# The last step of a fused attention and mixer kernel: blocks, writes and reads in another order, and one batch's products dealt otherwise

## The chip, the cores and the metric

The kernel runs on one core of one Trainium2 chip. The metric is device time in microseconds (us). The core has five engines, each with its own stream of instructions: TensorE (PE in the profile, its weight loads PEld), VectorE (DVE), ScalarE (ACT), GpSimd (POOL) and SyncE (SP). They meet through semaphores. SyncE and ScalarE also issue DMA transfers (SPq and ACTq in the profile); [...].

## The reference

For 8 batches and 8 heads, with a sequence of 576 and heads of 64, attention keeps the 32 largest scores of each row; then a mixer follows.

```python
scores = scale * np.matmul(q, k.transpose(0, 1, 3, 2))
kth = np.partition(scores, -top_k, axis=-1)[..., -top_k:-top_k + 1]
scores = np.where(scores >= kth, scores, -1000000000.0)
attn = np.exp(scores - np.max(scores, axis=-1, keepdims=True))
attn = attn / (np.sum(attn, axis=-1, keepdims=True) + 1e-09)
o = np.matmul(attn, v)
x = o.transpose(0, 2, 1, 3).reshape(B, S, H * D)          # 8 x 576 x 512
h = x.transpose(0, 2, 1) @ U @ V                          # rank 32 over the sequence
u = x + h.transpose(0, 2, 1)
out = u + np.maximum(u @ w_ch1, 0.0) @ w_ch2              # 512 -> 2048 -> 512
```

## The kernel before, in words

**Pairs, tiles and steps.** Two heads are a pair g (0 to 31, four to a batch). A pair has five tiles of rows: t = 0 to 3 with 128 rows, for both heads, and the tail t = 4 with the last 64 rows of both. From pair 4 on, tiles 3 and 4 share a step. So `steps` has 132 entries (`STEPS`), step 131 being tiles (31,3) and (31,4), and the big loop over n runs to 133: steps 132 and 133 are a drain, in which only the later stages of the last tiles are left.

**A tile's way.** Scores are made on TensorE (L350) a step ahead. `front` finds the 32nd largest score with VectorE's maximum and replace instructions; it is a generator whose stages the loop calls with `next(here)` in its own step and `next(last)` in the next: ScalarE computes what is to be masked (L571), GpSimd subtracts it (L572), ScalarE takes the exponentials with their sums (L453) and adds a small number to the sums, `den` (L582). `blocks` then turns a tile: VectorE transposes 32 x 32 blocks into `y` (L598), SyncE writes `y` to DRAM as `away` in four transfers (L604), and `back` has ScalarE issue the read of `away` into `PT` (L613), which completes the transposition. The tail is turned on TensorE by `turns` (L634, L639), with ScalarE's copies out of PSUM (L635, L640). `values` multiplies by v (L708, L711; the tail L682), two steps after the tile's own step in the drain (`weighted(n - 2)`), three steps after it otherwise, and ScalarE copies the result to `XT` (L720, L689).

**Sums and mixing.** `inverse` has VectorE invert a pair's sums (L651), transpose them (L653) and SyncE write them to DRAM as `rd` in four transfers (L657); `scale` has ScalarE issue two reads that spread them over partitions (L668). `mixed` multiplies a pair's values by these factors on GpSimd (L740, L743), transposes them (L750, L761), multiplies by U (L773) and V (L785), and GpSimd adds the result to `uT` (L801). It is a generator that goes on by one yield in each fill; its argument `wait` is the number of fills between L761's copy and L773.

**Fills.** `fill` deals out TensorE work of the mixer's two layers: it advances the mixing by one yield and then adds a share to `due` and takes products from `fillers` until the share is used up. In the drain the share is 1.02 and a product of 256 columns counts 0.5, so that a fill is two products, three now and then. `mlp(b)` makes a batch's products in two parts of columns: chunks 0, 1 and 4 (320 columns), then 2 and 3 (256 columns, `lo > 0`); each has 64 products of the first layer (L845) and, for each of four output chunks c, 16 of the second (L862). When 16 are done, ScalarE copies the sum (L873), GpSimd adds `uT` (L874), and `later(12, turned_back(...))` puts the store off by 12 products: TensorE transposes (L886), ScalarE copies (L888), SyncE stores (L892). Batch 6 (`B - 2`, the seventh) is the one in work during the drain; at the start of step 132's second fill, all that is left of it is c = 1, 2 and 3 of its second part, 48 products. The last batch, 7, is done after the drain by `closing`, in a form with fewer products but sums and differences on GpSimd (L931 to L934) and VectorE (L963 to L966); its products are at L938. It is called when pair 31's mixing has ended.

**Order in the drain.** [...] In step 132: fill, values of (31,1), fill, the exponentials of (31,3)'s first half, read of (31,2)'s blocks, two fills, the exponentials of (31,3)'s second half and of (31,4) with the sums, fill, inversion and reading of the factors, values of (31,2), fill, blocks of (31,3), two fills. In step 133: fill, tail's transposes, fill, read of (31,3)'s blocks, three fills, values of (31,3) and (31,4), and the mixing of pair 31 in the fills that follow.

Of the kernel before, what the change touches and what calls it, by code (L numbers as in the profile page):

```python
# [8 lines left out]
F32 = mybir.dt.float32  # L9
# [17 lines left out]
def kernel(  # L27
# [28 lines left out]
    nc = tc.nc  # L56
    B, H, S, D = q.shape
    P = 128
# [4 lines left out]
    NT, TAIL = 4, 64  # L63
    MAIN = NT * P
    HALF = S // 2
    assert S == MAIN + TAIL and D == 64 and H % 2 == 0 and C == 512 and TOPK % 8 == 0
    NPAIR = H // 2
    NP = B * NPAIR

    CH = NT + 1  # L70
    ALONE = NPAIR * CH
# [4 lines left out]
    BLK = 32  # L76
# [8 lines left out]
    mlpp = ctx.enter_context(tc.tile_pool(name="mlpp", bufs=2))  # L85
# [44 lines left out]
    def rows(t):  # L130
        return P if t < NT else TAIL
# [7 lines left out]
    def half(h):  # L139
        return slice(h * D, (h + 1) * D)  # L140
# [324 lines left out]
    def eased(g, t):  # L465
        return bool(ways(g, t)[2])

    def front(tiles):


# [139 lines left out]
    def back(g, t):  # L610

        if (g, t) in aways:
            nc.scalar.dma_start(  # L613
                PTs[g, t].rearrange("p a n -> p (a n)"),
                aways.pop((g, t)).rearrange("p a n -> p (a n)"),
            )
# [26 lines left out]
    def inverse(g, lo, hi):  # L643
        den = dens[g][:, lo:hi]
        if g == NPAIR - 1:
            nc.vector.tensor_scalar_add(den, den, 1e-9)
        if g < NPAIR:
            nc.vector.reciprocal(den, den)
            return
        inverted.add(g)  # L650
        nc.vector.reciprocal(upright[:, 0 : 2 * NT + 1], den)  # L651
        turned_ = small.tile([P, BLK], F32, tag="rows", name="rows", bufs=1)
        nc.vector.transpose(turned_, upright)  # L653
        rd = dram.tile([2 * NT + 1, P], F32, tag="rd", name="rd")
        scales[g] = rd
        for a in range(4):
            nc.sync.dma_start(  # L657
                rd[:, a * BLK : (a + 1) * BLK], turned_[a * BLK : a * BLK + 2 * NT + 1]
            )

    def scale(g):

        rd = scales.pop(g)
        sc = attn.tile([P, TAIL + S], F32, tag="scale", name="scale", bufs=1)
        scales[g] = sc
        flat = rd.rearrange("r n -> () (r n)")
        for h in range(2):
            nc.scalar.dma_start(  # L668
                sc[half(h), (1 - h) * TAIL : (1 - h) * TAIL + S],
                flat[:, h * S : (h + 1) * S].to_broadcast([D, S]),  # L670
            )
# [140 lines left out]
    def later(wait, job):  # L812

        posts.append((ticks + wait, job))

    def tick():

        nonlocal ticks
        ticks += 1
        if posts and posts[0][0] <= ticks:  # L820
            posts.pop(0)[1]()

    def first_layer(cc, f):

        at_ = f * P % W1Q
        return w1s[f * P // W1Q][:, cc, at_ : at_ + P]

    def mlp(b):

        uT = uTs[b]  # L830
        for chunks, (lo, hi) in zip(PARTS, SPAN):
            w = hi - lo
            hTs, phs = [], {}
            order = [(f, cc) for f in range(NF) for cc in range(NC)]
            if lo == 0:
                early = NC - 1
                order[0 : 2 * NC] = [(f, cc) for f in range(2) for cc in range(early)] + [
                    (f, early) for f in range(2)
                ]
            for f, cc in order:  # L840
                while cc == NC - 1 and b not in whole:
                    yield 0
                if cc == 0:
                    phs[f] = ps_m.tile([P, C], F32, tag="mm", name="mm")
                nc.tensor.matmul(  # L845
                    phs[f][:, 0:w],
                    lhsT=first_layer(cc, f),
                    rhs=uT[:, cc, lo:hi],
                    start=(cc == 0),
                    stop=(cc == NC - 1),  # L850
                )
                tick()
                if cc == NC - 1:
                    if f % 2 == 0:
                        hT = mlpp.tile([P, 2, WIDE], F32, tag="hT", name="hT", bufs=HT)
                        hTs += [hT[:, 0], hT[:, 1]]
                    nc.scalar.activation(hTs[f][:, 0:w], phs.pop(f)[:, 0:w], AF.Relu)  # L857
                yield w / C
            for c in range(NC):
                po = ps_m.tile([P, C], F32, tag="mm", name="mm")  # L860
                for f in range(NF):
                    nc.tensor.matmul(  # L862
                        po[:, 0:w],
                        lhsT=w2[:, f, c * P : (c + 1) * P],
                        rhs=hTs[f][:, 0:w],
                        start=(f == 0),
                        stop=(f == NF - 1),
                    )
                    tick()
                    if f < NF - 1:  # L870
                        yield w / C
                oT = mlpp.tile([P, WIDE], F32, tag="oT", name="oT")
                nc.scalar.copy(oT[:, 0:w], po[:, 0:w])  # L873
                nc.gpsimd.tensor_tensor(oT[:, 0:w], oT[:, 0:w], uT[:, c, lo:hi], ALU.add)  # L874
                later(12, turned_back(b, chunks, lo, c, oT))
                yield w / C

    def turned_back(b, chunks, lo, c, oT):


        def run():
            cs = slice(c * P, (c + 1) * P)
            tp = ps_t.tile([P, 3, P], F32, tag="tp", name="tp")
            for i, t in enumerate(chunks):
                n = rows(t)
                nc.tensor.transpose(tp[0:n, i, :], oT[:, OFF[t] - lo : OFF[t] - lo + n], ident)  # L886
            ob = mlpp.tile([P, 3, P], F32, tag="ob", name="ob", bufs=2)
            nc.scalar.copy(ob[:, 0:2], tp[:, 0:2, :])  # L888
            if NT in chunks:
                nc.scalar.copy(ob[0:TAIL, 2], tp[0:TAIL, 2, :])  # L890
            t = chunks[0]
            nc.sync.dma_start(  # L892
                out[b, 0:MAIN, cs].rearrange("(p t) c -> p t c", t=NT)[:, t : t + 2, :],
                ob[:, 0:2],
            )
            if NT in chunks:
                nc.sync.dma_start(out[b, MAIN:S, cs], ob[0:TAIL, 2])

        return run
# [259 lines left out]
    STEPS = len(steps)  # L1159
# [5 lines left out]
    fillers, mixing, due = [], [], 0.0  # L1165

    def fill(k=1):


        nonlocal due  # L1170
        for _ in range(k):
            if passes:
                passes.pop(0)()
            if mixing and next(mixing[0], True):
                mixing.pop(0)
            part = share * (LONG if len(tiles(n)) > 1 else 1)
            if n <= ALONE + BATCH + 2:
                part *= EARLY[min(max(n - ALONE, 0) // NT, NT - 1)]
            due += part
            while due > 0:  # L1180
                if not fillers:
                    due = 0.0
                    break
                done = next(fillers[0], None)
                if done is None:
                    fillers.pop(0)
                elif not done:
                    due = 0.0
                else:
                    due -= done  # L1190

    def tiles(n):

        return steps[n] if 0 <= n < STEPS else []

    def weighted(m):

        for g, t in tiles(m):
            values(g, t)
        if tiles(m)[-1][1] == NT:  # L1200
            mixing.append(mixed(g, None, 1 if g > NPAIR + 1 else 4) if m < STEPS - 1 else mixed(g, 5, 0))

    def turn():

        for _ in tiles(n - 2):
            next(turning, None)

    def turned(n):

        for g, t in tiles(n):  # L1210
            yield from turns(g, t)
# [3 lines left out]
    t = 0  # L1215
# [5 lines left out]
    for n in range(STEPS + 2):  # L1221
        if n < STEPS:
            g, t = steps[n][0]
# [8 lines left out]
        else:  # L1232
            t = NT
# [81 lines left out]
                scores(*tile_, len(tiles(n + 1)) > 1)  # L1315
            fold(*tile_)
        turn()
        fill()
        turn()
        next(last, None)  # L1320
        for tile_ in tiles(n - 2):
            back(*tile_)
        fill()
        turn()
        fill()
        next(last, None)
        if n < STEPS and n - 2 >= ALONE and len(tiles(n - 2)) > 1:
            scale(steps[n - 2][0][0])
        next(here, None)
        if g == NPAIR:  # L1330
# [1 line left out]
        fill()  # L1332
        if n >= STEPS:
            if n == STEPS:
                inverse(NP - 1, 0, 2 * NT + 1)
                scale(NP - 1)
            weighted(n - 2)
        next(here, None)
        for tile_ in tiles(n + 1):
# [4 lines left out]
            if shared(*tile_):  # L1344
                blocks(*tile_)
        turning = turned(n - 1)
        if n < STEPS and n - 1 >= ALONE and len(tiles(n - 1)) > 1:
            owed.append(steps[n - 1][0][0])
            if owed[0] > NPAIR + 1:
                inverse(owed.pop(), 0, 2 * NT + 1)  # L1350
# [45 lines left out]
```

## Time and profile before

| what | us |
|---|---|
| median of 3 runs | 1650.82 (1650.72 to 1653.34) |
| the profiled execution | 1653.27 |
| its span, first to last instruction | 1651.5 |
| TensorE busy | 1558.9 (94%) |
| VectorE busy | 1543.5 (93%) |
| ScalarE busy | 993.8 (60%) |
| GpSimd busy | 1009.1 (61%) |
| values of (31,1), (31,2), (31,3) begin | 1503.62, 1510.31, 1520.86 |
| closing products of batch 7 begin | 1535.60 |
| last product ends | about 1646 |

A line of instructions in order of time gives start, duration, engine, line of the source, operation, what it writes and reads with their shapes, and how many such instructions are merged in it; in brackets at the end stands how long the engine was idle before it and what ended the wait. Rows of digits are the busy share in tenths, in 40 equal slices of the span. A matrix product in 32-bit floats shows as two records. ACTq and SPq lines are the issue of a DMA, not its transfer.

### The profile page before, as it was taken

The numbers are of one execution on the slowest core, as the hardware profiler recorded it, in microseconds if no ns is written. First come the engines' busy times: TensorE is split into PE (matmuls) and PEld (weight loads), VectorE is DVE, ScalarE is ACT, GpSimd is POOL, SyncE is SP. The second block draws the span as 40 slices with busy tenths as digits, with TensorE's granted clock in tenths as the row PEclk, the third lists the DMA queues.
The fourth block names the chain that finished last, engine by engine and source line by source line (L and its number), as shares of the span: only waits on it lengthen the run. The fifth ranks groups of instructions, "written<-read, shape, count | busy, mean of one in ns | idle before, by whom it ended". The sixth has DMA issues, their size and how long they took to land.

```text
span 1651.5 us, 30266 instructions
## 1 busy us (share of the span) xinstructions
PE 1558.9 (94%) x9656; PEld 1185.5 (72%) x9656; DVE 1543.5 (93%) x4388; ACT 993.8 (60%) x2481; POOL 1009.1 (61%) x881
## 2 busy tenths in 40 slices
PE   4566799999999999999999999999999999999998
PEld 2344466788667877788777877788777877787776
DVE  7999999999999999999999999999999999994452
ACT  4888787665665556565666656565655556563320
POOL 4888767756666666665666566656666565653720
PEclk7787799999999999999999999999999999999999
DMA  3333331145445455555545455555545455543001
GB/s 89 100 99 99 88 83 36 42 113 136 135 120 146 126 142 145 134 135 132 138 120 143 129 140 142 140 134 132 137 121 143 128 140 137 142 125 100 7 1 28
DMA packets 278959, 187.06 MB, mean 113 GB/s; under 512 B 174128, under 2 KB 259984, under 8 KB 278800
## 3 DMA queue, kind: packets, MB, share of 16 engines
q1 hardware_dynamic: 258576, 116.44, 29.3%
q10 hardware_dynamic: 20224, 68.69, 13.1%
q8 instruction: 76, 1.25, 0.3%
q14 instruction: 83, 0.68, 0.1%
HBM read 115.31 MB, written 69.73 MB: 112 GB/s over the span
## 4 chain that ended last, share of the span: by engine, by line
PE 72%; DVE 13%; POOL 5%; ACT 4%; DMA 2%; SPq 1%; issue 1%; DVEq 0%; ACTq 0%; POOLq 0%
PE mm L862 22%; PE mm L845 21%; PE sc L350 7%; PE O L711 6%; DVE m L539 4%; DVE upper L534 3%; PE mm L938 3%; PE up L785 2%; PE tp L938 2%; PE sc L938 2%; PE sc L382 2%; PE O L708 1%; PE tp L634 1%; DVE first L521 1%; DVE upper L502 1%; POOL E L544 1%
## 5 line engine op out<-in xcount | busy, mean ns | idle before, releaser
L845 PE MATMUL mm<-uT,w 128*128 128x320 f32 (+1 forms) x1792 | 461.1, 408 | 2.6 <-POOL uT L801 2.1
L862 PE MATMUL mm<-hT,w 128*128 128x320 f32 (+1 forms) x1792 | 460.6, 408 | 0.0
L572 POOL TENSOR_TENSOR Ssb<-Ssb,E 128x576 f32<-128x576 f32 x243 | 339.7, 1418 | 192.4 <-ACT E L571 192.4
L845 PEld LDWEIGHTS mm<-uT,w 128*128 128x128 f32 x1792 | 333.1, 190 | 102.5 <-issue 9.6
L862 PEld LDWEIGHTS mm<-hT,w 128*128 128x128 f32 x1792 | 332.0, 190 | 91.6 <-issue 9.8
L539 DVE MAX8 m<-upper 128x8 f32<-128x304 f32 (+1 forms) x774 | 362.5, 509 | 0.7
L534 DVE MATCH_REPLACE8 upper<-m,upper 128x304 f32<-128x304 f32 (+1 forms) x516 | 256.6, 504 | 0.0
L449 POOL TENSOR_TENSOR lower<-lower,upper 128x576 uint32<-128x576 uint32 x108 | 152.4, 1411 | 135.9 <-DVE upper L448 134.0
L446 POOL TENSOR_TENSOR lower<-Ssb 128x576 uint32<-128x576 uint32 x108 | 152.4, 1411 | 125.6 <-ACT Ssb L395 60.7
L453 ACT ACTIVATE Ssb<-Ssb,nmax 128x576 f32<-128x576 f32 x258 | 201.8, 784 | 18.2 <-POOL Ssb L545 9.2
L350 PE MATMUL sc<-qkT 64*128 64x288 f32 (+1 forms) x1056 | 178.5, 460 | 8.8 <-ACT Ssb L404 7.6
L571 ACT ACTIVATE E<-Ssb,least 128x576 f32<-128x576 f32 x243 | 176.2, 768 | 4.2
L502 DVE MAX8 upper<-lower 128x8 f32<-128x288 f32 x432 | 171.8, 438 | 1.7 <-POOL lower L449 1.7
L395 ACT COPY Ssb<-sc 128x576 f32<-128x576 f32 x216 | 127.5, 642 | 72.7 <-PE sc L350 72.6
L598 DVE STREAM_TRANSPOSE y<-Ssb 128x512 f32<-128x512 f32 (+1 forms) x306 | 150.9, 543 | 0.0
L711 PE MATMUL O<-PT,va 128*64 128x128 f32 x2048 | 144.2, 284 | 0.0
L857 ACT ACTIVATE hT<-mm 128x320 f32<-128x320 f32 (+1 forms) x224 | 91.1, 407 | 82.5 <-PE mm L845 76.9
L350 PEld LDWEIGHTS sc<-qkT 64*128 64x128 f32 (+1 forms) x1056 | 95.4, 196 | 49.8 <-issue 18.0
L711 PEld LDWEIGHTS O<-PT,va 128*64 128x64 f32 x2048 | 112.9, 140 | 16.2 <-issue 1.6
L720 ACT COPY XT<-O 128x128 f32<-128x128 f32 x128 | 33.9, 265 | 107.2 <-PE O L711 100.4
L534 DVE MATCH_REPLACE8 upper<-first,upper 128x304 f32<-128x304 f32 x216 | 97.5, 458 | 0.0
L500 DVE MATCH_REPLACE8 lower<-upper,lower 128x288 f32<-128x288 f32 x216 | 93.9, 442 | 0.0
(268 smaller groups left out, 2270.9 us busy)
## 6 DMA issues: line engine op xcount, KB each, us to landing
away<-y SPq DMA_DIRECT2D x408, 144.0 KB
PT<-away ACTq DMA_DIRECT2D x102, 576.0 KB
raw<-in_moe_w_ch_dram SPq DMA_DIRECT2D x32, 512.0 KB
va<-in_v_dram SPq DMA_DIRECT2D x64, 128.0 KB
scale<-rd ACTq DMA_DIRECT2D x56, 144.0 KB
out_dram<-ob SPq DMA_DIRECT2D x59, 128.0 KB
ld<-in_q_dram SPq DMA_DIRECT2D x108, 64.0 KB
ld<-in_k_dram SPq DMA_DIRECT2D x108, 64.0 KB
```

The costliest lines, as they stand in the source:

```text
L350: nc.tensor.matmul(out, lhsT=qkT[half(h), 0, cols(t)], rhs=qkT[half(h), 1, lo:hi], start=True, stop=True,)
L446: nc.gpsimd.tensor_tensor(bottom, a.bitcast(U32), b.bitcast(U32), ALU.add)
L449: nc.gpsimd.tensor_tensor(bottom, bottom, top.bitcast(U32), ALU.subtract)
L453: nc.scalar.activation(E, chunk, AF.Exp, bias=nmax, scale=SCALE, accum_out=total)
L502: nc.vector.max(spot, lower)
L534: nc.vector.match_replace(nxt, ms[c], curs[c], NEG)
L539: nc.vector.max(ms[c], curs[c])
L571: nc.scalar.activation(gap, chunk, AF.Relu, bias=least[:, c : c + 1], scale=-WIDEN)
L572: nc.gpsimd.tensor_tensor(chunk, chunk, gap, ALU.subtract)
L711: nc.tensor.matmul(O[half(h)], lhsT=va[:, h, j, :], rhs=PT[:, NT * h + j], start=False, stop=(j == NT - 1),)
L845: nc.tensor.matmul(phs[f][:, 0:w], lhsT=first_layer(cc, f), rhs=uT[:, cc, lo:hi], start=(cc == 0), stop=(cc == NC - 1),)
L862: nc.tensor.matmul(po[:, 0:w], lhsT=w2[:, f, c * P : (c + 1) * P], rhs=hTs[f][:, 0:w], start=(f == 0), stop=(f == NF - 1),)
```

## The change

The order of the drain's work is changed, and the stores of batch 6's last part.

- In step 132 the read of (31,2)'s blocks comes after all exponentials, two more fills stand ahead of (31,2)'s values, and the inversion of pair 31's sums comes after the blocks of (31,3). The factors are read in step 133, after (31,3)'s blocks.
- In step 133 three fills are left out (`pace` does nothing there), and the mixing of pair 31 waits 3 fills instead of 5 ahead of its product with U.
- In batch 6's second part of columns, the store of c = 0 is put off by 20 products instead of 12. Those of c = 1, 2 and 3 are turned by VectorE in blocks of 32 x 32 and stored by eight transfers each (`blocked_store`), in place of two transposes on TensorE, a copy on ScalarE and one transfer.

```diff
-                later(12, turned_back(b, chunks, lo, c, oT))
+                later(20 if b == B - 2 and lo > 0 and c == 0 else 12, turned_back(b, chunks, lo, c, oT))
...
+    def blocked_store(b, c, chunks, ob, at_=0):
+
+        for a in range(4):
+            cs = slice(c * P + a * BLK, c * P + (a + 1) * BLK)
+            for i, t in enumerate(chunks):
+                nc.sync.dma_start(
+                    out[b, 0:MAIN, cs].rearrange("(m i t) c -> t i m c", i=BLK, t=NT)[t],
+                    ob[a * BLK : (a + 1) * BLK, at_ + i * P : at_ + (i + 1) * P].rearrange(
+                        "i (m c) -> i m c", c=BLK
+                    ),
+                )
+
     def turned_back(b, chunks, lo, c, oT):
         def run():
+            if b == B - 2 and lo > 0 and c > 0:
+                ob = mlpp.tile([P, 3 * P], F32, tag="ob", name="ob", bufs=2)
+                nc.vector.transpose(ob[:, 0 : 2 * P], oT[:, 0 : 2 * P])
+                blocked_store(b, c, chunks, ob)
+                return
...
+    def pace():
+
+        if n <= STEPS:
+            fill()
...
-            mixing.append(mixed(g, None, 1 if g > NPAIR + 1 else 4) if m < STEPS - 1 else mixed(g, 5, 0))
+            mixing.append(mixed(g, None, 1 if g > NPAIR + 1 else 4) if m < STEPS - 1 else mixed(g, 3, 0))
...
         turn()
-        fill()
+        pace()
         turn()
         next(last, None)
-        for tile_ in tiles(n - 2):
-            back(*tile_)
-        fill()
+        if n != STEPS:
+            for tile_ in tiles(n - 2):
+                back(*tile_)
+        pace()
         turn()
-        fill()
+        pace()
         next(last, None)
-        if n < STEPS and n - 2 >= ALONE and len(tiles(n - 2)) > 1:
+        if n == STEPS:
+            for tile_ in tiles(n - 2):
+                back(*tile_)
+        if n - 2 >= ALONE and len(tiles(n - 2)) > 1:
             scale(steps[n - 2][0][0])
...
             if n == STEPS:
-                inverse(NP - 1, 0, 2 * NT + 1)
-                scale(NP - 1)
+                fill(2)
             weighted(n - 2)
...
-        if n < STEPS and n - 1 >= ALONE and len(tiles(n - 1)) > 1:
+        if n - 1 >= ALONE and len(tiles(n - 1)) > 1:
             owed.append(steps[n - 1][0][0])
             if owed[0] > NPAIR + 1:
                 inverse(owed.pop(), 0, 2 * NT + 1)
```

## The prediction

> **What bounds the kernel now.** I read the page first, then TensorE's instructions in order of time through the drain (loop steps 132 and 133, about 1503 to 1536 us), then ScalarE's and SyncE's there, then busy time by stretch. From the page, the busy shares and the end of the chain by line:
>
> ```profile
> PE 1558.9 (94%) x9656; PEld 1185.5 (72%) x9656; DVE 1543.5 (93%) x4388; ACT 993.8 (60%) x2481; POOL 1009.1 (61%) x881
> PE   4566799999999999999999999999999999999998
> DVE  7999999999999999999999999999999999994452
> ```
>
> VectorE is full until slice 37 and idle half of the time after it; TensorE is full to the end. Nothing in the diff acts before step 132, so only the drain and what follows can move. TensorE there:
>
> ```profile
> 1503.62 0.39 PE L708 MATMUL O<-PT,vd 128*128 128x128 f32 x2
> ...
> 1504.95 4.15 PE L862 MATMUL mm<-hT,w 128*128 128x256 f32 x18
> 1510.31 0.49 PE L708 MATMUL O<-PT,vd 128*128 128x128 f32 x2 [1.20 <-DMA PT<-away]
> ...
> 1515.53 0.60 PE L634 MATMUL tp<-ident,Stail 128*128 128x128 f32 x4
> ...
> 1516.07 3.62 PE L862 MATMUL mm<-hT,w 128*128 128x256 f32 x16
> 1520.86 0.46 PE L708 MATMUL O<-PT,vd 128*128 128x128 f32 x2 [1.17 <-DMA PT<-away]
> ```
>
> A product of batch 6 (256 columns) is two records: 16 records in 3.62 us, of which 0.17 is the last one's modelled tail, make 0.431 us per product. Counted so, TensorE is free at 1504.95 + 9 x 0.431 = 1508.83 and starts tile (31,2)'s values at 1510.31: wait A, 1.48 us. It is free again at 1516.07 + 8 x 0.431 = 1519.52 and starts (31,3)'s at 1520.86: wait B, 1.34 us. Both are for blocks read back from DRAM. A third, wait C, stands at the head of batch 7's closing products:
>
> ```profile
> 1540.75 1.13 PE L938 MATMUL mm<-Stail,raw 128*128 128x288 f32 x4
> 1542.48 0.44 PE L886 MATMUL tp<-ident,oT 128*128 128x128 f32 x2 [0.59 <-POOL oT L874]
> ```
>
> The closing products start at 1535.60; the 12 up to 1542.48 need 12 x 0.485 = 5.82 us, so 1.06 us is lost (0.76 at the store's transpose, 0.30 before it). After that the stretch 1542.5 to 1647.5 has TensorE busy 104.45 of 105 us. The end is therefore TensorE's work plus A + B + C = 3.88 us, and this is nearly all that can be won. What ScalarE does between:
>
> ```profile
> 1506.79 0.33 ACTq L613 DMA_DIRECT2D PT<-away  x1
> 1507.17 0.78 ACT L453 ACTIVATE Ssb<-Ssb,nmax 128x576 f32<-128x576 f32 x1 [1.06 <-POOL Stail L572]
> ...
> 1508.83 0.30 ACT L582 ACTIVATE den<-den,eps 128x9 f32<-128x9 f32 x1
> 1511.97 1.12 ACTq L668 DMA_DIRECT2D scale<-rd  x2
> ...
> 1516.64 0.27 ACT L640 COPY PTt<-tp 128x128 f32<-128x128 f32 x1
> 1517.07 0.32 ACTq L613 DMA_DIRECT2D PT<-away  x1
> ```
>
> ScalarE stands until 1506.79 for the write of (31,2)'s blocks, and the exponential that (31,3)'s blocks need starts only then. VectorE inverts the sums at 1509.16 to 1509.62 and transposes the blocks at 1509.59 to 1511.09; SyncE issues the sums' rows, then the blocks.
>
> [...]read (31,3) is issued at 1517.07, just after its blocks landed at 1516.97. [...]in step 129 the read at 1471.90 precedes the start (1472.13) of the copy L640 that the program has ahead of it. [...]here reads of blocks took 2.1 to 3.0 us of packets, alone or with other traffic.
>
> **The change part by part.**
>
> *Read (31,2)* goes behind the exponentials of (31,3) and the tail. The last of these that waits is the tail's, for GpSimd's subtraction, which ends at 1506.84. I put the issue at 1507.1 (before: 1506.79); the bound, if it has to stand behind the sums' addition, is 1508.1. Issue to first product took 3.52 us, so it is ready at 1510.62, or 1510.75 with the next blocks' write beside it.
>
> *Two fills* before these values: 4 products more, so TensorE arrives at 1504.95 + 13 x 0.431 = 1510.55. Wait A becomes 0.2 us: -1.28. Bounds of A: 0 and 1.2.
>
> *Blocks (31,3).* Their exponential no longer waits: 1506.1 to 1506.97 (0.87 as before). VectorE transposes at 1507.05 to 1508.55, SyncE issues 4 writes by 1510.4, and with 3.7 us from transpose to landing (1502.96 to 1506.64 for (31,2)), and up to 1.2 for the collision with the read, they land by 1513.5, 3.5 us earlier. The inversion (0.43 us of VectorE) and 4 row writes (1.35 us of SyncE) come after: rows land by 1514. Batch 6's first late store is put off to the 20th product, so it can't stand in SyncE ahead of them.
>
> *Read (31,3)* doesn't get these 3.5 us. In step 133 it stands on ScalarE behind the copies L635 and L640 of tile (31,4), which wait for TensorE's transposes L634 and L639, and these stand behind three fills of step 132 and one of step 133. TensorE: 1510.75 + 1.44 (values) + 8 x 0.431 + 0.22 (the put-off store's two transposes) = 1515.86. From L634 to the read took 0.88 to 0.94 us in the steps before (1470.96 or 1471.02, by the modelled start, to 1471.90), so 1516.74. From issue to first product, 3.79 us as before: 1520.53. Three fills are gone from step 133, so TensorE is there at 1515.86 + 0.54 + 2 x 0.431 = 1517.26. Wait B becomes 3.27 us: +1.93. Bounds 2.7 to 3.9. The stall that the earlier write should cure moves behind a transpose.
>
> *Factors.* Their read (2 DMAs) now follows read (31,3). In step 129 its packets end 4.7 us after the block read's issue, so it lands about 5.0 after: 1521.75. GpSimd then needs 2.16 us for four multiplications, 1523.9; TensorE wants the result at 1520.53 + 2.0 + 4 x 0.431 = 1524.25. The slack is 0.3 us; I charge +0.2, bounds 0 and 1.5.
>
> *Batch 6's stores c = 1 to 3*: 6 transposes at 0.11 leave TensorE, -0.66, and 3 copies (0.37) ScalarE. Added are three VectorE transposes of 256 columns, about 0.43 each (0.48 for 288 columns in L1123), where VectorE is otherwise idle 22.9 us, and 24 writes of 16 KB, about 0.43 us of SyncE each, where SyncE has nothing queued from 1544 to 1608. Nothing on the path. If that cover were gone, 3 x 8 x 0.43 = 10.3 us of SyncE would delay later stores.
>
> *Wait of 3 instead of 5 fills, three fills fewer in step 133.* The products aren't removed: 11 instead of 5 stand after the mixing's last transforms. So 2.6 us more of cover for GpSimd's sums and VectorE's differences, which bound the closing's head: wait C goes, -1.06; bounds -0.5 and -1.06. The copies between (1.4 us) still fit in 3 fills (2.6 us).
>
> Sum: -1.28 + 1.93 + 0.2 - 0.66 - 1.06 = -0.87. The profiled execution took 1653.27 us (span 1651.5 and 1.8 around it), so it would be 1652.4; its runs had a median of 1650.82, which gives **1649.9 us**. With the bounds of all terms: -1.48 + 1.36 - 0.66 - 1.06 = -1.84 to -0.28 + 2.56 + 1.5 - 0.66 - 0.5 = +2.6, so 1649.0 to 1653.4 is the forecast's own range. 0.2% (3.3 us) is about what a measurement of this kernel tells from no change; runs before already spread 2.6.
>
> **Rivals.**
>
> *Both block waits vanish* (0.12). If ScalarE gives out read (31,3) as soon as the blocks have landed (1513), it is ready at 1516.8, before TensorE's 1517.26. B is then 0: -1.28 - 1.34 - 0.66 - 1.06 = -4.3, 1646.5 us. For it speaks that reads overtake queued copies; against it, that I find no read that passes an instruction still waiting for its semaphore.
>
> *A stays* (0.14). The read is issued at 1508.1, ready at 1511.7: A is 1.1 and all after it moves by 0.9; 1650.8 us. [...]for it, that four queued instructions are more than the usual lead.
>
> *The factors' read becomes the bound: slower* (0.08). Place: TensorE at transpose L750, for GpSimd's multiplications. Each us that the factors land after about 1522.0 costs one. Slower by over 0.2% needs 4.2 us beyond that, 1526.2, over 9 us after the issue. For it: the read was ahead by half a step and hidden, and now it is behind 576 KB in its own queue, beside a 128 KB store. Against it: in step 129 the pair is done in 5 us. It would give 1654.5 or more.
>
> *The forecast itself* has 0.66.
>
> **How the numbers follow.** The forecast and "A stays" both lie within 0.2%: 0.80 same. Faster is the first rival, 0.12; slower the third, 0.08. The range of 8 in 10 leaves out most of the first and third and takes in the bounds short of their joint extremes and the spread of runs: 1647.4 to 1652.6.
>
> **What would show it.** Right: read (31,2) at about 1507 and A under 0.5; writes of blocks (31,3) from about 1508.6; read (31,3) some 0.9 us after L634, and B near 3.3, the longest idle time of TensorE in the drain; closing products from about 1535.8 with no wait after. Wrong: a read issued before L634 (B gone); L750 waiting for GpSimd; closing products that still wait for sums, or VectorE idle behind a store's transposes.

## The result and the profile after

The changed kernel takes 1654.68 us (median of 13 runs, 1653.35 to 1656.53), the kernel before 1650.97 (13 runs). The ratio is 1.0019, with a 95% interval of 1.0010 to 1.0027: slower by 3.7 us, of which the interval leaves 1.7 to 4.5. The forecast was 1649.9, and 1654.68 lies outside its range of 1647.4 to 1652.6.

The two profiled executions reach the drain at different times: the values of (31,1) begin at 1503.62 before and at 1501.41 after, and the change does nothing ahead of step 132. So all that follows is counted from there. From there to the first closing product it is 31.98 us before and 35.92 after, +3.94; to the end of the span 147.88 and 150.39, +2.51. TensorE after, in order of time; the lines that were 708, 634, 750 still are, the closing's L938 is now L955:

```profile
1501.41 0.38 PE L708 MATMUL O<-PT,vd 128*128 128x128 f32 x2
...
1502.75 5.88 PE L862 MATMUL mm<-hT,w 128*128 128x256 f32 x26
1510.02 0.49 PE L708 MATMUL O<-PT,vd 128*128 128x128 f32 x2 [1.39 <-DMA PT<-away]
...
1515.24 0.60 PE L634 MATMUL tp<-ident,Stail 128*128 128x128 f32 x4
...
1515.79 1.03 PE L862 MATMUL mm<-hT,w 128*128 128x256 f32 x4
1520.59 0.67 PE L708 MATMUL O<-PT,vd 128*128 128x128 f32 x2 [3.77 <-DMA PT<-away]
1521.18 1.98 PE L711 MATMUL O<-PT,va 128*64 128x128 f32 x16
...
1537.33 1.13 PE L955 MATMUL sc<-uT,w 128*128 128x288 f32 x4
```

Wait A, counted as in the prediction: TensorE is free at 1502.75 + 13 x 0.431 = 1508.35 and starts at 1510.02, 1.67 us (1.48 before). Wait B: free at 1515.79 + 0.86 = 1516.65, starts at 1520.59, 3.94 us (1.34 before). And something that before doesn't have: the 16 records of L711 take 1.98 us instead of 1.09, and both tiles' values 3.57 us (1520.59 to 1524.16) instead of 2.00. Busy time by stretch shows why; the columns are the stretch, its length, the busy time of PE, PEld, DVE, ACT and POOL with their instructions, then the granted clock, DMA share and GB/s:

```profile
1517.34:1520.75 3.41, 0.16 (x1) 0.19 (x2) 0.00 (x0) 0.00 (x0) 0.00 (x0) 0.99 0.78 235
1520.75:1524.16 3.41, 3.41 (x38) 3.07 (x38) 0.00 (x0) 0.27 (x1) 0.69 (x1) 0.51 0.15 48
```

After a stretch of 3.41 us in which TensorE was busy for 0.16, the granted clock is half for as long again. The closing products have lost wait C: the first 12 of them run from 1537.33 on at their 0.97 us per four records (two products), with no idle time. ScalarE after, and GpSimd's first use of the factors:

```profile
1505.57 0.30 ACT L582 ACTIVATE den<-den,eps 128x9 f32<-128x9 f32 x1
1505.71 0.33 ACTq L613 DMA_DIRECT2D PT<-away  x1
...
1515.88 0.58 ACT L635 COPY PTt<-tp 128x512 f32<-128x512 f32 x1 [0.50 <-PE tp L634]
1516.13 0.33 ACTq L613 DMA_DIRECT2D PT<-away  x1
1516.36 0.27 ACT L640 COPY PTt<-tp 128x128 f32<-128x128 f32 x1
1516.62 4.34 ACTq L668 DMA_DIRECT2D scale<-rd  x2
```

```profile
1523.47 1.43 POOL L740 TENSOR_TENSOR uT<-XT,scale 128x256 f32<-128x256 f32 x2 [9.23 <-DMA scale<-rd]
```

The sum to the first closing product: A +0.19, B +2.60, values +1.57, the products after them +0.1, the transposes gone from this stretch -0.44: +4.0, and +3.94 is measured. From the closing on the prediction's working has wait C and the last two transposes, -1.06 - 0.22 = -1.28, so +2.7 for +2.51 measured.

### The profile page after: what moved, and what is told of

Same layout as the page of the kernel before. It is cut to its first block, busy times and chain, and to the rows that moved or that the text cites. A ratio compares the mean times of both kernels' runs of the same rounds, so it can differ in the third digit from the quotient of the medians.

```text
span 1651.8 us, 30279 instructions
## 1 busy us (share of the span) xinstructions
PE 1556.6 (94%) x9650; PEld 1183.9 (72%) x9650; DVE 1543.9 (93%) x4391; ACT 992.9 (60%) x2478; POOL 1009.5 (61%) x881
## 4 chain that ended last, share of the span: by engine, by line
PE 72%; DVE 22%; DMA 2%; issue 1%; SPq 1%; ACT 1%; DVEq 0%; ACTq 0%
PE mm L862 22%; PE mm L845 22%; DVE m L539 7%; DVE upper L534 7%; PE sc L350 7%; PE O L711 6%; PE mm L955 3%; DVE first L521 2%; PE tp L955 2%; PE sc L955 2%; PE up L785 2%; PE sc L382 2%; DMA PT<-away 2%; PE O L708 1%; PE tp L634 1%; DVE upper L502 1%
## 5 line engine op out<-in xcount | busy, mean ns | idle before, releaser
L711 PE MATMUL O<-PT,va 128*64 128x128 f32 x2048 | 143.7, 284 | 0.0
L711 PEld LDWEIGHTS O<-PT,va 128*64 128x64 f32 x2048 | 112.4, 140 | 16.1 <-issue 1.3
```

Of the source, the lines that this page charges most:

```text
L711: nc.tensor.matmul(O[half(h)], lhsT=va[:, h, j, :], rhs=PT[:, NT * h + j], start=False, stop=(j == NT - 1),)
```

## The experiments

Every ratio is against the kernel before, run on the same chip at the same time. "Changed" stands for the changed kernel, +3.7 us.

**TensorE kept busy in wait B.** 30 transposes that nobody reads, ahead of the values of (31,3):

```diff
             if n == STEPS:
                 fill(2)
+            else:
+                spin = ps_s.tile([P, 2, 512], F32, tag="sc", name="sc")
+                for _ in range(30):
+                    nc.tensor.transpose(spin[:, 0, 0:P], ident, ident)
             weighted(n - 2)
```

> The changed kernel, with 30 transposes of the identity into an unused accumulator (about 3.3 us of TensorE work that nobody reads) ahead of the values of (31,3) in step 133, so that TensorE does not stand still while it waits for the read. Theory 1 (the long wait makes the granted clock drop to half, and the values then run at half speed): no half-clock stretch in the drain, values of (31,3) and (31,4) take 2.0 us instead of 3.57, still starting about 19.2 us after the values of (31,1); the run is 1.6 us faster than the changed kernel, so about 2 us slower than before. Theory 2 (the transfers that run at that time slow the values): they still take about 3.5 us, and the time stays that of the changed kernel, 3.7 us over before.

Measured: 1653.03 us for 1650.85, ratio 1.0015 (1.0009 to 1.0022), +2.2 us. TensorE in that run, in order of time:

```profile
1516.75 3.44 PE L1365 MATMUL sc<-ident 128*128 128x128 f32 x30
1520.64 0.46 PE L708 MATMUL O<-PT,vd 128*128 128x128 f32 x2 [0.45 <-DMA PT<-away]
1521.03 1.09 PE L711 MATMUL O<-PT,va 128*64 128x128 f32 x16
...
1524.46 0.95 PE L750 MATMUL tp<-ident,uT 128*128 128x128 f32 x4
1525.64 0.30 PE L761 MATMUL tp<-ident,uT 128*64 128x128 f32 x1 [0.23 <-POOL uT L743]
```

The values start 19.19 us after those of (31,1), as in the changed kernel (19.18), with the same transfers beside them, and take 2.0 us. So it is the clock, not the transfers, that slows the values: theory 2 falls. Work added to the idle engine made the kernel 1.5 us faster by the medians. In the profiled executions it is 0.8 us from the values of (31,1) to the first closing product (35.12 for 35.92), and not 1.57: at the mixing's transposes TensorE now waits for GpSimd, which waits for the factors. L761 follows 1.18 us after the start of L750, in the changed kernel 0.44.

**How long a wait brings the half clock.** The same with 6 and with 15 transposes:

> As the run with 30 transposes of the identity ahead of the values of (31,3), but with 6 (0.66 us), so that some 3.3 us of the second wait are left, about what the prediction had for it. [...]it falls in some executions and not in others: 0 to 1.6 us faster than the changed kernel (3.7 us over before), a median between 2.1 and 3.7 us over before. If any wait over 3 us brings it, the time is the changed kernel's[...].

> The same with 15 transposes (1.65 us): some 2.3 us of the wait are left. No half clock; values in 2.0 us; about 2.1 us over before, as with 30. Rival: the half clock comes after waits of 2.3 us too, and it is 3.7 us over before.

Measured: 1654.10 for 1651.00 with 6 (1.0020, 1.0014 to 1.0027; +3.1 us), and 1653.70 with 15 (1.0015, 1.0008 to 1.0023; +2.7). Both profiled executions have the half clock: the 16 records of L711 take 1.98 and 1.72 us. Columns as above: two stretches of the run with 15 transposes; two, later in the drain, of the run below with the factors after the values; and two of the run with 30, far ahead of the drain:

```profile
1519.17:1522.58 3.41, 1.29 (x14) 0.96 (x14) 0.00 (x0) 0.00 (x0) 0.00 (x0) 1.00 0.71 208
1522.58:1525.99 3.41, 3.41 (x38) 3.13 (x33) 0.00 (x0) 0.48 (x2) 1.30 (x2) 0.50 0.16 48
```

```profile
1526.88:1530.29 3.41, 1.62 (x8) 1.10 (x9) 0.00 (x0) 0.78 (x2) 2.00 (x4) 1.00 0.00 0
1530.29:1533.70 3.41, 3.41 (x9) 2.72 (x9) 0.00 (x0) 0.05 (x1) 0.00 (x0) 0.50 0.00 0
```

```profile
419.23:422.64 3.41, 1.72 (x10) 0.77 (x6) 3.41 (x11) 2.63 (x6) 3.17 (x3) 1.00 0.72 193
422.64:426.05 3.41, 3.12 (x11) 2.00 (x12) 3.41 (x11) 1.73 (x5) 0.92 (x2) 1.00 0.41 154
```

My expectation missed for 15: with 2.1 us of idle time left, and TensorE busy for 38% of the stretch, the clock fell in this execution. With 6, where 3.25 us of the wait are left, it fell too, and the median, +3.1, lies between the 2.1 and 3.7 expected for a clock that falls in some executions only.

The traces say more than these two runs. In that of the changed kernel half clock begins at 192.92, 1520.70 and 1650.41, and 1327.78 and 129.71 us are 389 and 38 times 3.413; in that of the kernel before, at 194.62 and 1652.12, 427 times 3.413 apart. So the stretches lie on a grid in each of these two traces, and on another in each. Cut on it, from 205 us on, they have three stretches at full clock that half clock followed: TensorE was busy there for 0.11 us (from 1517.29) and 0.55 (from 1647.00) in the changed kernel, and not at all before (from 1648.70). It followed none of the others, which have 1.66 us (49%, from 1645.29 before) or more. In the runs shown it followed 1.29 us with 15 transposes, 1.62 (47%) with the factors after the values, and not 1.72 with 30. So 1.79 us of idle time in one stretch brought it, in several waits of which the longest counts 1.31 there, and 1.75 us did not. Ahead of 205 us, where the program starts, it is less clean: in the kernel before, half clock followed 1.90 us (from 146.84), and not 1.77 (from 119.54). A wait of 2.12 us brought it in the execution with 15 transposes; whether it would in each was not measured. The medians (+3.7 with none, +3.1, +2.7, +2.2 with 30) go down with the wait that is left, but their intervals overlap.

**The three fills of step 133 put back.**

```diff
     def pace():
-        if n <= STEPS:
-            fill()
+        fill()
```

> The changed kernel, with the three fills of step 133 put back. Theory 1 (what is lost is the wait for read (31,3), bare of cover, and the clock after it): that wait falls from 3.94 to about 1.4 us, no half-clock stretch, values in 2.0 us; 4.2 us faster than the changed kernel, so 0.5 to 1.7 us faster than before. Theory 3 (the loss is in the stores in blocks or the order of the closing part): it stays more than 1 us slower than before.

Measured: 1651.00 for 1650.85, ratio 1.0000 (0.9992 to 1.0008). The second wait is 1.27 by the record and the values take 2.0 us, so the loss against before is gone, as theory 1 has it, and theory 3 falls. The gain over before that I expected is not there, though. TensorE shows where part of it went:

```profile
1523.88 0.38 PE L750 MATMUL tp<-ident,uT 128*128 128x128 f32 x2
1524.42 0.44 PE L750 MATMUL tp<-ident,uT 128*128 128x128 f32 x2
1525.09 0.30 PE L761 MATMUL tp<-ident,uT 128*64 128x128 f32 x1 [0.23 <-POOL uT L743]
```

The transposes of the mixing wait for GpSimd, which waits for the factors: L761 follows 1.21 us after the start of L750, where before it followed after 0.44 (1524.91 to 1525.35), so 0.8 us. Another 0.4 us is lost at L955, where the third pair of closing products waits for GpSimd's sums, as it doesn't in the changed kernel: the three fills are no longer there to cover them. Wait A is as long as ever.

**Read (31,3) at the start of step 133.**

```diff
+        if n > STEPS:
+            for tile_ in tiles(n - 2):
+                back(*tile_)
         next(last, None)
         fill()
...
-        if n != STEPS:
+        if n < STEPS:
             for tile_ in tiles(n - 2):
                 back(*tile_)
```

> The changed kernel, with read (31,3) issued at the start of step 133, ahead of its first fill and of the tail's copies. Theory 1 (the read stands behind copies that wait for TensorE): it is issued 2.9 us earlier, about 11.8 us after the values of (31,1) begin, the wait ahead of the values of (31,3) falls from 3.94 to 1.0 us or less, no half clock; 4.5 to 5 us faster than the changed kernel, so 1 to 2 us faster than before. Rival: the blocks have not landed by then or ScalarE's stand delays the tail's copies; the wait stays over 2.5 us and the gain is under 1.5 us.

Measured: 1649.69 for 1650.85, ratio 0.9990 (0.9982 to 0.9999), 1.2 us faster than before. Nothing but the place of one DMA issue in ScalarE's order differs from the changed kernel. ScalarE and then TensorE in that run:

```profile
1513.20 0.33 ACTq L613 DMA_DIRECT2D PT<-away  x1
1516.13 0.47 ACTq L668 DMA_DIRECT2D scale<-rd  x1
```

```profile
1515.25 0.60 PE L634 MATMUL tp<-ident,Stail 128*128 128x128 f32 x4
...
1517.11 0.46 PE L708 MATMUL O<-PT,vd 128*128 128x128 f32 x2 [0.28 <-DMA PT<-away]
1517.49 1.09 PE L711 MATMUL O<-PT,va 128*64 128x128 f32 x16
```

The read leaves ahead of L634, 11.8 us after the values of (31,1) begin; the wait is 0.28 us by the record, and the clock stays. That the earlier blocks were held up by the tail's copies is thereby shown. The gain isn't larger because the factors are late here too: L750 begins 0.3 us late and L761 follows 1.36 us after it, 1.2 us in all.

**Store of c = 1 put off behind the closing's differences.**

```diff
-later(20 if b == B - 2 and lo > 0 and c == 0 else 12, turned_back(b, chunks, lo, c, oT))
+later((20, 26, 12, 12)[c] if b == B - 2 and lo > 0 else 12, turned_back(b, chunks, lo, c, oT))
```

> The changed kernel, with the store of c = 1 of batch 6 put off to the 26th product, so that VectorE turns it behind the closing's differences. Theory 4 (the eight small-packet writes beside read (31,3) delay its landing): from issue to first value 3.8 us instead of 4.46, the wait 3.3 us; 0.6 us faster than the changed kernel, 2 us if the wait gets short enough to keep the clock. Rival: the read takes as long as in the changed kernel and the time is the same within 0.3 us.

Measured: 1654.65 for 1650.85, ratio 1.0023 (1.0014 to 1.0031). The small writes moved from 1515.93 (changed) to 1538.31, and the read still takes 4.58 us from issue (1516.29) to first value (1520.87), in the changed kernel 4.46. Theory 4 falls.

**Factors after the values of (31,3):**

```diff
-        if n - 2 >= ALONE and len(tiles(n - 2)) > 1:
+        if n < STEPS and n - 2 >= ALONE and len(tiles(n - 2)) > 1:
             scale(steps[n - 2][0][0])
...
             weighted(n - 2)
+            if n > STEPS:
+                scale(NP - 1)
```

> The changed kernel, with the factors' read issued after the values of (31,3), so that nothing follows read (31,3) in ScalarE's queue. The mixing then waits for the factors, so the total is of no interest. Theory 6 (the factors' read behind it is what made read (31,3) slow to be seen): from issue to first value 3.8 us instead of 4.46. Rival: it stays at 4.4 or more. Also whether a second wait of about 3.3 us still brings the half clock.

Measured: 1658.5 us, a single run. The read takes 4.24 us (1515.73 to 1519.97): between the two expectations. In the seven executions with the factors' read right behind it, it took 4.42 to 4.60 us, 4.58 of them without the small writes. In the four others where TensorE waited for it, it took 3.79 to 4.24: 3.79 before, 3.91 in the run with this read moved, 4.01 in the run with only the stores changed, and 4.24 here, these last two with the small writes beside it. So the factors' read behind it adds some tenths of a microsecond; whether the small writes add anything where it is gone isn't settled by single executions. The half clock was there again after the second wait of 3.7 us, and once more after the wait for the factors (the stretch from 1526.88 shown above).

**Read (31,2) back in its old place**, ahead of the second exponentials:

```diff
-        if n != STEPS:
-            for tile_ in tiles(n - 2):
-                back(*tile_)
+        for tile_ in tiles(n - 2):
+            back(*tile_)
...
-        if n == STEPS:
-            for tile_ in tiles(n - 2):
-                back(*tile_)
```

> The changed kernel, with read (31,2) back in its old place, ahead of the exponentials of (31,3)'s second half. Theory 5 (the first wait did not shrink because the read stands behind the sums' addition on ScalarE and runs beside the write of (31,3)'s blocks): the read is issued about 3.2 us after the values of (31,1) begin instead of 4.3, takes 3.5 us to its first value instead of 4.3, and the first wait falls from 1.67 to under 0.3 us. The second wait and the half clock stay, since the second read hangs on the tail's copies: about 1.5 us faster than the changed kernel. Rival: the first wait falls but the second grows by as much, time unchanged.

Measured: 1653.15 for 1651.02, ratio 1.0010 (1.0003 to 1.0016), +2.1 us, so 1.6 faster than changed. ScalarE and TensorE in that run:

```profile
1504.48 0.33 ACTq L613 DMA_DIRECT2D PT<-away  x1
1506.52 0.30 ACT L582 ACTIVATE den<-den,eps 128x9 f32<-128x9 f32 x1
```

```profile
1508.34 0.38 PE L708 MATMUL O<-PT,vd 128*128 128x128 f32 x2
...
1518.80 0.77 PE L708 MATMUL O<-PT,vd 128*128 128x128 f32 x2 [3.77 <-DMA PT<-away]
```

Wait A is gone, and wait B is as long as in the changed kernel: the second read hangs on TensorE's own transposes, so it moves along with them (it leaves 0.88 us after L634, at 1514.34). In this execution the half clock lasted 6.83 us, two stretches.

**Only the stores of c = 1 to 3**, on the kernel before: `turned_back` and `blocked_store` as in the change, nothing else.

> The kernel before, with only the stores of c = 1 to 3 of batch 6's second part done in blocks by VectorE. Its part of the prediction: 6 transposes leave TensorE (-0.66 us) and the store's transpose in the closing products no longer waits for GpSimd (-0.76): 1.0 to 1.5 us faster than before. Rival (VectorE or the 24 small writes cost what is won): the same within 0.4 us.

Measured: 1649.83 for 1651.02, ratio 0.9992 (0.9983 to 1.0000), 1.2 us faster: this part does what the prediction said of it, though the interval ends at no change. From the values of (31,1) to the end it is 146.65 us for 147.88.

**Both reads placed anew.** The changed kernel with read (31,2) in its old place, read (31,3) at the start of step 133 and the factors' read between the put-off store's copy and the tail's:

```diff
+        if n > STEPS:
+            for tile_ in tiles(n - 2):
+                back(*tile_)
         next(last, None)
         fill()
...
+        if n > STEPS:
+            scale(NP - 1)
         turn()
         pace()
         turn()
         next(last, None)
-        if n != STEPS:
+        if n <= STEPS:
             for tile_ in tiles(n - 2):
                 back(*tile_)
...
-        if n == STEPS:
-            for tile_ in tiles(n - 2):
-                back(*tile_)
-        if n - 2 >= ALONE and len(tiles(n - 2)) > 1:
+        if n < STEPS and n - 2 >= ALONE and len(tiles(n - 2)) > 1:
```

> The changed kernel with both reads placed anew: read (31,2) in its old place, read (31,3) at the start of step 133, and the factors' read between the put-off store's copy and the tail's copies. If the account of waits holds: first wait under 0.3 us, second under 0.6, no half clock, closing products without a wait: 3.5 to 4.5 us faster than before. Rival: the earlier reads make the factors the last arrival, TensorE waits for GpSimd at the transposes of the mixing, and it is no better than the run with only read (31,3) moved, 1.2 us faster than before.

Measured: 1647.66 for 1651.02, ratio 0.9979 (0.9969 to 0.9989): 3.4 us faster than before, and some 7 faster than the changed kernel. TensorE:

```profile
1508.55 0.38 PE L708 MATMUL O<-PT,vd 128*128 128x128 f32 x2
...
1515.53 0.46 PE L708 MATMUL O<-PT,vd 128*128 128x128 f32 x2 [0.29 <-ACT PTt L640]
...
1530.69 1.13 PE L955 MATMUL sc<-uT,w 128*128 128x288 f32 x4
```

No wait A, a B of 0.46 us (1514.21 + 0.86 to 1515.53) that is now for a copy of ScalarE, no wait at L750 or in the closing. By the account, with this B put in, it should win 1.48 + (1.34 - 0.46) + 1.06 + 0.66 = 4.1 us; from the values of (31,1) to the end it is 143.6 us for 147.88, 4.3 less.

## Why the prediction was wrong

The account that the end is TensorE's work plus its waits in the drain holds: in the changed kernel it adds up to within 0.1 us up to the closing, and for the best kernel it foretold 3.5 to 4.5 us, of which the medians show 3.4 and the profiled executions 4.3. Two steps of it failed, and one price was missing. Times are from the start of the values of (31,1).

1. **"Wait A becomes 0.2 us: -1.28"** failed: it is 1.67. TensorE arrives at 6.94 us, as worked out (6.93). But the read was put at 3.48 (1507.1), on my estimate that only instructions waiting for another engine hold it, for which I had no more than one copy passed in step 129; it left at 4.30, 0.14 us after the sums' addition L582 began, close to the bound that I had given (1508.1, or 4.48) and set aside. It also takes 4.31 us to the first value instead of 3.52, and for running beside the write of (31,3)'s blocks only 0.13 had been charged. In the trace its packets take 2.95 us instead of 2.22, and the last 0.85 of them lie beside that write; that the write is the cause is likely, but wasn't tried alone. The case "A stays" was the nearest on this point, with an A of 1.1. With the read in its old place A is 0.

2. **"Wait B becomes 3.27 us: +1.93"** had the mechanism right and the size wrong. The blocks are turned 3.27 us after the start (3.43 foretold), their packets end at 9.7 (landing foretold by 9.9), and the read leaves 0.89 us after L634 (0.88): the gain of the earlier write is lost behind the tail's copies, which the run with the read moved shows. The mis-sized term is the time from issue to first value: I took 3.79 from before, where the factors' read went ahead; with the factors' read behind it, it took 4.46. B is 3.94, 0.67 more.

3. **No step priced what a wait of this length does to the clock**: 1.57 us on the values and 0.1 behind them. The working turned 1.3 us of wait into 3.3 and counted each microsecond once. In the changed kernel half clock followed a stretch of 3.41 us with 0.11 us of TensorE work, and lasted 3.41 us. Waits of 3.25 and 2.12 us brought it in the runs with 6 and with 15 transposes, so the forecast's 3.27 us was not safe either.

4. **The stores and the closing (-0.66, -1.06)** were right: the stores made 1.2 us alone, and no wait is left in the closing. The stores alone leave a wait of 0.4 us at L955, as does the run with the fills put back; so the fills moved behind the mixing do their part. That their writes have "nothing queued" beside them was not: VectorE turned c = 1 at 1514.28 and its eight writes began at 1515.93, beside read (31,3), not behind the values (1520.59). Moving them away changed nothing that could be measured.

5. **The factors (+0.2)** cost nothing in the changed kernel: L750 did not wait. That was luck. They were put at 5.0 us after the block read's issue, and GpSimd starts on them 7.34 us after it (1523.47), since their two issues last until 1520.96; only because the values were late and slow too did nobody wait. Where those losses go, they cost 0.7 to 0.8 us (30 transposes, fills put back), and 1.2 us with the read moved. The rival of a slower kernel rested on them, so it did not foresee the result. The rival that both waits vanish became true only in the kernel that moves the reads.

Sum: -0.87, +1.47 for A, +0.67 for B, +1.67 for the clock, -0.2 for the factors make +2.7; the profiled executions give +2.5. The medians give +3.7. The rest is within the interval. That some executions lose a second stretch to the half clock, as one did in the run with read (31,2) moved, would fit, but isn't shown for the changed kernel.

## What to carry to other kernels

Here read (31,3) left at 1516.13 behind the tail's copies, though the packets of its blocks had ended at 1511.1, and at 1513.20 in the run with its issue ahead of them. Before counting on an earlier producer, follow the order of the engine that issues the transfer back to whatever it waits for, here TensorE's own transposes, behind which the wait came back. When a change gathers short waits of TensorE into one, price the clock after it too: here one wait of 3.9 us cost another 1.6. Useful work dealt into the wait won the loss back (1651.00 for 1650.85), and even useless work paid (1.5 us). Where the DMA issues stand mattered most: three moved ones (both block reads and the factors) made 7 us between the changed and the best kernel.

## What was not expected of the hardware

- The half clock followed stretches of 3.41 us on a grid in which TensorE was busy for 47% or less (0.11 and 0.55 us in the changed kernel, 1.29 with 15 transposes, 1.62 with the factors after the values), and not those with 1.66 us (49%, before) or 1.72 (30 transposes). After 1.62 us no single wait in the stretch was over 1.31 us. In the drain it lasted 3.41 us in the changed kernel and 6.83 with read (31,2) in its old place.
- The factors' two issues on ScalarE, 1.1 us together before, took 4.3 to 4.5 us in the six profiled runs where read (31,3) had just been issued and SyncE was issuing the eight writes of c = 1. They took 1.1 us where the writes had been moved away, and where the read left earlier. What holds the second one back was not tried.
